# A fused attention and feed-forward kernel: a sixth VectorE exp buffer, residual rows loaded in place, and a wait that keeps GpSimd behind two-port operations

## The chip, the cores and the metric

The kernel runs on one core of one Trainium2 chip. The metric is the device time of that core in microseconds, the median of several executions. The program is built by a scheduler inside the kernel's source: it walks over streams of operations, decides which engine does what next, and emits one fixed instruction list for each engine. "Order" below means that order; it is fixed when the program is built, and it does not adapt on the chip. The program lets engines wait for each other only at semaphores.

## The reference, cut to what matters

```python
# x: 2048 rows of 512, 32 heads of 16, feed-forward width 1792, bfloat16
h  = x + attention(layernorm(x)) @ wo        # softmax over 2048 keys for each row and head
h2 = h + (gelu(n @ w_gate) * (n @ w_up)) @ w_down   # n = layernorm(h)
```

The softmax needs an exp for 32 x 2048 x 2048 scores. Cut into tiles of 128 x 512, that is 2048 tiles.

## The kernel before: the parts that matter

Most tiles go to ScalarE, two per instruction. The rest go to VectorE in groups of four: four evacuations from PSUM to 16-bit integers, and a chain of three wide operations in which GpSimd does a quarter of the product. The two factors that remain in X and W are then both multiplied with V by TensorE.

```python
# ScalarE: two tiles per exp
yield Op("act", TEXP(n), ACTF(PT[:, p0:p0 + n, :], pbank[:, b0:b0 + n, :], ACT.Exp, ...), ...)

# VectorE: one evacuation per tile (x4)
yield Op("dve", 0.603, lambda e: e.tensor_scalar(out=dXE[k % NX][:, 0, j, :], in0=pbank[:, b, :], ...))
...
# VectorE, once per group of n = 4: mask, product of 3 tiles; GpSimd: product of the 4th; second mask
yield Op("dve", ..., lambda e: e.tensor_scalar(out=W, in0=X, scalar1=0x3ff, scalar2=0xb800, ...), port=True)
yield Op("dve", ..., lambda e: e.tensor_tensor(out=W[:, 0:nd, :], in0=W[:, 0:nd, :], in1=X[:, 0:nd, :], op=ALU.mult), port=True)
yield Op("pool", TPOOL, lambda e, j=j: e.tensor_tensor(out=W[:, j, :], in0=W[:, j, :], in1=X[:, j, :], op=ALU.mult), port=True)
yield Op("dve", ..., lambda e: e.tensor_scalar(out=X, in0=X, scalar1=0x7c00, scalar2=0x8, ...), port=True)
```

`port=True` marks operations of VectorE and GpSimd that the scheduler plans one after the other, but only in its own clock. VectorE's are called two-port operations from here on; that is a name. On the chip, a GpSimd operation begins when the semaphores of its own operands allow it: all of the 369.2 us for which GpSimd is idle before its products end with VectorE's product (L1730 in the trace). GpSimd's product also lists W's first tile among its reads, so it does wait for VectorE's product of the same group; nothing keeps it behind the wide operations of other groups:

```python
def _emit(self, op, start):
    ...
    if op.port:
        self.port = end            # the plan: the next port user begins here
    ...
    tok = P.op(op.eng, fn, reads=op.reads, writes=op.writes, ...)   # semaphores: data only
```

The residual rows of x have a buffer of their own, two rows of tiles deep:

```python
xres = at("xres", [128, 2, D], BF16)
...
yield Op("dve", 0.605, lambda e: e.tensor_tensor(out=hh[:, qt, :], in0=pbank[:, b2, :], in1=xres[:, xi, :], op=ALU.add), ...)
```

Of the kernel before, what the change touches and what calls it, by code (L numbers as in the profile page):

```python
# [891 lines left out]
class Sched:  # L892
# [5 lines left out]
    def __init__(self, P, banks):  # L898
        self.P = P
        self.t = {n: 0.0 for n in P.ENGINES}  # L900
        self.done = {}
        self.streams = []
        self.banks = [(0.0, b) for b in banks]
        self.now = 0.0
        self.fill = None
        self.debt = (0.0, 0.0)
        self.pipe = 0.0
        self.lent = set()
        self.rng = random.Random(66)
        self.early = True  # L910
        self.wake = None
        self.port = 0.0
        self.room = lambda: False
        self.mode = "f"
        self.rows = [0.0] * 4
        self.due = self.INF
# [61 lines left out]
    def _emit(self, op, start):  # L978
        if op.cols:
            self.owed(start + op.dur, op.cols)  # L980
        P = self.P
        extra = op.extra() if op.extra else ()
        for tok in extra:
            start = max(start, self.done[tok] + LATS.get((tok[0], op.eng), LAT))
        self.now = max(self.now, start)
        if op.eng == "pe":
            m = "r" if op.mode == "q" else op.mode
            if m != self.mode:
                start = max(start, max(self.rows)) + TSW
            self.mode = m  # L990
        end = start + op.dur
        last = end
        if op.gs:
            at = start
            for g in op.gs:
                at = max(at, self.rows[g])
                self.rows[g] = at + TST
                at += 0.005
            end, last = at, max(self.rows)
        if op.port:  # L1000
            self.port = end
        if op.dma is not None:
            tok = P.dma(op.eng, op.fns[0], op.dma, reads=op.reads, writes=op.writes, extra_deps=extra)
            self.t[op.eng] = start + 0.5
            self.pipe = max(start + 1.5, self.pipe) + op.dur / 0.32
            self.done[tok] = self.pipe + 0.8
            if op.dma[0] in TURNS:
                self.t[op.eng] = start + 1.25
                self.done[tok] += TURNS[op.dma[0]]
        else:  # L1010
            if op.eng == "pe":
                self.wake = None
                P.group_begin("pe")
            n = len(op.fns)
            for i, fn in enumerate(op.fns):
                tok = P.op(op.eng, fn, reads=op.reads, writes=op.writes, sig=(i == n - 1), extra_deps=extra)
            if op.eng == "pe":
                P.group_end("pe")
            self.t[op.eng] = end
            self.done[tok] = last + TAIL.get(op.eng, 0.0)  # L1020
        if op.then is not None:
            op.then()
# [128 lines left out]
GS = 4  # L1151
NPOOL = 1
TPOOL = 1.11
NX = 5
GLAST = 8
AHEAD = 12
ATAIL = 8
# [10 lines left out]
XMIN = 32768.0  # L1168
# [48 lines left out]
def fast_path(nc, P, base0, ARENA, pbank, flag, A_x, A_wqkv, A_wo, B_x, B_w_gate, B_w_up, B_w_down, out):  # L1217
# [58 lines left out]
    wo_sb = at("wo_sb", [128, 4, D], BF16)  # L1276
    OnT = at("OnT", [128, 4, 4, 128], BF16)
    hn_sb = OnT[:].rearrange("p q c s -> p q (c s)")
    xres = at("xres", [128, 2, D], BF16)
    ident = at("ident", [128, 128], BF16)  # L1280
    ident32 = at("ident32", [128, 128], FP32)
    ones_bf = at("ones_bf", [128, 512], BF16)
    zero_bf = at("zero_bf", [128, 128], BF16)
    stats = at("stats", [128, NT, 6], FP32)
    mv = at("mv", [128, NT, 2], FP32)
# [83 lines left out]
        return ("x", 0, t // 2) if c == 0 else ("x", c)  # L1369

    def consts():
        yield Op("pool", 0.5, lambda e: e.memset(ones_bf[:], 1.0), writes=["ones_bf"])
        yield Op("pool", 0.3, lambda e: e.affine_select(out=ident[:], in_=ones_bf[:, 0:128], pattern=[[1, 128]], compare_op=ALU.is_equal, fill=0.0,
                                                        base=0, channel_multiplier=-1), reads=["ones_bf"], writes=["ident"])
        yield Op("pool", 0.1, lambda e: e.memset(nhalf[:], -0.5), writes=["nhalf"])
        yield Op("pool", 0.2, lambda e: e.memset(LINV[:], 2.0 ** -10), writes=[("LINV", u) for u in range(NU)])
        yield Op("pool", 0.1, lambda e: e.memset(zero_bf[:], 0.0), writes=["zero_bf"])
        yield Op("pool", 0.3, lambda e: e.tensor_copy(out=ident32[:], in_=ident[:]), reads=["ident"], writes=["ident32"])

    def ones_v():  # L1380
        yield Op("dve", 0.62, lambda e: e.memset(VA[:, :, :, 16:17], 1.0), writes=["VA_ones"])
# [2 lines left out]
    def masks():  # L1384
        yield Op("dve", 0.5, lambda e: e.memset(pbank[:, DENSE[0], :], 0.0), writes=[("pb", DENSE[0])])
        for par in range(2):
            iv = ident32[:].rearrange("p (g x i) -> p g x i", g=4, x=2)[:, :, par, :]
            yield Op("dve", 0.2, lambda e, iv=iv, par=par: e.tensor_reduce(out=qmask[:, par:par + 1], in_=iv, axis=AX.XY, op=ALU.add), reads=["ident32"], writes=[("qm", par)])
            yield Op("dve", 0.1, lambda e, par=par: e.tensor_scalar(out=qmask[:, par:par + 1], in0=qmask[:, par:par + 1], scalar1=256.0 / LN2, scalar2=None, op0=ALU.mult),
                     reads=[("qm", par)], writes=[("qm", par)])  # L1390
        yield Op("dve", 0.1, lambda e: e.tensor_scalar(out=probe[:, 0:1], in0=ident32[:, 0:1], scalar1=1e6, scalar2=XMIN, op0=ALU.add, op1=ALU.max), reads=["ident32"], writes=["probe"])


    def ln1(c):
# [198 lines left out]
    def qk():  # L1593
        nxt, an = 0, 0
        while nxt < len(TILES):
# [11 lines left out]
            while nxt in own:  # L1607
# [3 lines left out]
            yield Op("pe", TST * repeats([TILES[i][2] for i, _ in put]), mode="q", cols=143 * len(put), gs=[TILES[i][2] for i, _ in put], fns=fns, reads=rd, writes=[("pb", b) for _, b in put],  # L1611
                     gate=lambda: C["exp"] >= st - len(SLOTS) + 1 and not sch.lent & {b for _, b in put})
            sch.wake = {TILES[i][2] for i, _ in put}
            C["qk"] = st + 1
            while nxt in own:
                nxt += 1
# [39 lines left out]
    def dget():  # L1656
# [8 lines left out]
        while True:  # L1665
            yield Wait(lambda: "qkdone" in C or (room() and find()))
            if "qkdone" in C:
                return
            u, i0 = find()
            G = C["gopen"] = dict(u=u, t=[], row=range(i0, i0 + 4), k=C["gk"], conv=0)  # L1670
            for i in G["row"]:
                own[i] = ("d", G["k"])
            C["gk"] += 1
            C["dnext"] = sch.now + DGAP
            while len(G["t"]) < GS:
                b = yield Acquire(gate=lambda: pick(G) is not None and C["dout"] < DMAX - (DB if behind() else 0))
                i = pick(G)
                C["dout"] += 1
                fns, rd = scores([(i, b)])
                wk = sch.wake | {TILES[i][2]}  # L1680
                yield Op("pe", TDQ if TILES[i][2] not in sch.wake else TST, mode="r", cols=143, gs=[TILES[i][2]], fns=fns, reads=rd, writes=[("pb", b)])
                sch.wake = wk
                sch.add(dconv(G, len(G["t"]), b), -2)
                G["t"].append(i)
            close_group()
# [181 lines left out]
    def base_dl(c):  # L1867
        return T0 + first_t[c + 1] * 2 * TUNIT + 10

    def xres_loads(c):  # L1870
        for t in range(first_t[c], first_t[c + 1]):
            yield Op("sp", 0.125, lambda e, t=t: e.dma_start(out=xres[:, t % 2, :], in_=xv[:, t, :]), writes=[("xres", t % 2)], dma=("xres", t % 2),
                     gate=lambda: C["oproj"] >= t - 1)


    def copy_op(c, qt, o, i, **kw):

# [3 lines left out]

    def post(c, qt):
        cp, t = 0, first_t[c] + qt
        xi = t % 2
        hh, hT = h_c[c], hnT_c[c]
        rd = [("Otok", cp, s) for s in range(NSLOT)] + ["ident"]
        if c < NC - 1:
# [11 lines left out]
        for hf in range(2):  # L1899
            yield Op("pe", 2 * TMM, cols=1024, fns=[MM(pbank[:, b2, :], OnT[:, qt, hc, :], wo_sb[:, hc, :], hc == 0, hc == 3) for hc in (2 * hf, 2 * hf + 1)],  # L1900
                     reads=[("OH", qt), "wo"], writes=[("pb", b2)])
        dQ = P.retire(h_over[c])
        yield Op("dve", 0.605, lambda e: e.tensor_tensor(out=hh[:, qt, :], in0=pbank[:, b2, :], in1=xres[:, xi, :], op=ALU.add),
                 reads=[("pb", b2), ("xres", xi)], writes=[("h", c, qt)], extra=lambda: dQ)
        sch.release(b2)
        C["oproj"] += 1
        yield Op("dve", 0.605, lambda e: e.bn_stats(out=stats2[:, t, :], in_=hh[:, qt, :]), reads=[("h", c, qt)], writes=[("stats2", t)])
# [175 lines left out]

    def warm():
        while "qk" not in C and sch.t["pe"] < 12:
            yield Op("pe", 0.43 if sch.t["pe"] < 5.2 else 0.22, lambda e: e.matmul(pbank[:, 0, :], ident[:], ones_bf[:], start=True, stop=True), reads=["ident", "ones_bf"], writes=[("pb", 0)],
                     gate=lambda: "qk" not in C and sch.t["pe"] < 12)

    def fill_op(b):
        return Op("pe", TMM, lambda e: e.matmul(pbank[:, b, :], zero_bf[:], ones_bf[:], start=False, stop=False, skip_group_check=True), reads=["zero_bf", "ones_bf"], writes=[("pb", b)], cols=390)  # L2090

    def fill(st, nxt):

# [3 lines left out]
            op = fill_op(C["pvb"])  # L2097
        elif sch.banks:
            b = min(sch.banks)[1]
            op = Op("pe", TMM, lambda e: e.matmul(pbank[:, b, :], zero_bf[:], ones_bf[:], start=True, stop=True), reads=["zero_bf", "ones_bf"], writes=[("pb", b)], cols=390)  # L2100
        else:
            return False
        t0 = max(sch.free("pe", op), sch._ready(op))
# [75 lines left out]
```

## Time and profile before

| | before |
|---|---|
| median of four executions | 814.68 us (814.17 to 814.97) |
| exps on ScalarE, and median spacing from end to end | 778, 0.917 us |
| sum of the spacings that end in an exp | 737.2 us |
| of it above 778 x 0.9165 us ("lost between exps") | 24.1 us |
| everything else in the profiled execution of 814.4 us | 77.2 us |
| two-port operations held up by a running GpSimd operation | 64, 22.7 us |

The last rows were worked out from the trace's single instructions; a "spacing" is the time from one instruction's end to the next one's on the same engine. "Held up" means: when VectorE had finished its previous operation and the wide one had begun, a GpSimd operation was running. Where "the first 40 us" or "40 to 780 us" is said, the count starts at TensorE's first clock record, 5.3 us after the span's start here.

The chain of waits of the kernel before is followed back from the last instruction, and gives the share of the span by engine, then by line:

```profile
PE 49%; DVE 30%; ACT 10%; issue 5%; POOL 2%; DMA 0%; DVEq 0%; ACTq 0%; POOLq 0%
PE pbank L1341 31%; PE pbank L1340 14%; DVE dXE L1715 12%; ACT PT L1347 8%; DVE dXE L1730 5%; DVE dXE L1728 4%; PE pbank L2090 4%; DVE dXE L1735 4%; DVE GUT L1981 1%; POOL dXE L1732 1%; ACT GUT L1994 1%; DVE OA L1819 1%; DMA xnT<-xn_sb 0%; ACT L1347 0%; POOL xn_sb L1442 0%
```

VectorE holds 30% of the chain, nearly all of it in the operations of the exp groups (L1715, L1728, L1730, L1735). PE's shares are in large part TensorE working through its list in order. A late VectorE makes TensorE late, and ScalarE then waits for scores. The list of waits says the same (who waited for whom: us in all, times, longest):

```profile
PEld pbank L1341 <- DVE dXE L1715: 36.9, 110, 1.2
...
PEld pbank L1341 <- DVE dXE L1735: 11.5, 33, 1.2
ACT PT L1347 <- PE pbank L1341: 10.2, 21, 1.7
```

### The profile page before, as it was taken

To read this page: it belongs to the slowest core of one execution; us is meant where nothing else is said; L and a number is where in the kernel's file an instruction comes from. 1 tells how busy PE (TensorE), PEld (TensorE's weight loads), DVE (VectorE), ACT (ScalarE), POOL (GpSimd) and SP (SyncE) were. 2 spreads that over 40 slices of the span, in tenths; PEclk is the share of its full clock that TensorE was granted. 3 is DMA by queue.
4 is the path that set the end of the run, shared out by engine and by line. 5 is a ranking of instruction groups with operands and counts; after the bars stand their busy time and mean duration, and the time that the engine had idled before them with its cause. 6 is when DMAs were issued, how large, how long until landed. Compare 5 with 4: busy or idle time off the path is not lost.

```text
span 812.7 us, 20343 instructions
## 1 busy us (share of the span) xinstructions
PE 792.2 (97%) x8342; PEld 276.0 (34%) x8342; DVE 758.9 (93%) x1236; ACT 769.8 (95%) x815; POOL 246.6 (30%) x283
## 2 busy tenths in 40 slices
PE   8999999999999999999999999999999999999998
PEld 4222222222222222222233333333443343444557
DVE  8679999999999999999999999999999999999965
ACT  5899999999999999999999999999999999999972
POOL 3513345532343222122143232223224222233210
PEclk9999999999999999999999999999999999999999
DMA  6200000610021000010011000010001100110000
GB/s 208 52 8 1 7 8 7 252 48 8 7 53 28 8 7 1 8 28 21 23 46 30 11 9 21 14 28 27 8 21 28 27 8 8 28 29 16 15 22 19
DMA packets 50022, 24.33 MB, mean 30 GB/s; under 512 B 39296, under 2 KB 48896, under 8 KB 49920
## 3 DMA queue, kind: packets, MB, share of 16 engines
q1 hardware_dynamic: 49776, 22.88, 10.8%
q8 instruction: 67, 1.10, 0.5%
q14 instruction: 35, 0.29, 0.1%
q10 hardware_dynamic: 144, 0.07, 0.0%
HBM read 11.80 MB, written 2.10 MB: 17 GB/s over the span
## 4 chain that ended last, share of the span: by engine, by line
PE 49%; DVE 30%; ACT 10%; issue 5%; POOL 2%; DMA 0%; DVEq 0%; ACTq 0%; POOLq 0%
PE pbank L1341 31%; PE pbank L1340 14%; DVE dXE L1715 12%; ACT PT L1347 8%; DVE dXE L1730 5%; DVE dXE L1728 4%; PE pbank L2090 4%; DVE dXE L1735 4%; DVE GUT L1981 1%; POOL dXE L1732 1%; ACT GUT L1994 1%; DVE OA L1819 1%; DMA xnT<-xn_sb 0%; ACT L1347 0%; POOL xn_sb L1442 0%
## 5 line engine op out<-in xcount | busy, mean ns | idle before, releaser
L1347 ACT ACTIVATE PT<-pbank 128x1024 bf16<-128x1024 f32 x778 | 724.1, 1080 | 13.4 <-PE pbank L1341 10.2
L1341 PE MATMUL pbank<-QT,KT 32*128 32x512 bf16 (+1 forms) x2304 | 346.9, 359 | 8.4 <-DVE dXE L1715 3.3
L1715 DVE TENSOR_SCALAR dXE<-pbank 128x512 uint16<-128x512 f32 x492 | 323.0, 680 | 8.8 <-PE pbank L1341 6.7
L1732 POOL TENSOR_TENSOR dXE<-dXE 128x512 f16<-128x512 f16 x123 | 155.3, 1263 | 369.2 <-DVE dXE L1730 369.2
L1341 PEld LDWEIGHTS pbank<-QT,KT 32*128 32x128 bf16 x2304 | 89.2, 91 | 294.3 <-ACT PT L1347 201.9
L1341 PE MATMUL pbank<-PT,VA 128*32 128x256 bf16 (+2 forms) x2708 | 130.1, 292 | 0.0
L1730 DVE TENSOR_TENSOR dXE<-dXE 128x1536 f16<-128x1536 f16 x123 | 122.1, 993 | 1.1
L1728 DVE TENSOR_SCALAR dXE<-dXE 128x2048 uint16<-128x2048 uint16 x123 | 94.3, 767 | 0.1
L1735 DVE TENSOR_SCALAR dXE<-dXE 128x2048 uint16<-128x2048 uint16 x123 | 88.1, 720 | 5.8 <-POOL dXE L1732 4.8
L1341 PE MATMUL pbank<-dXE,VA 128*32 128x256 f16 (+2 forms) x1752 | 76.2, 289 | 2.0 <-DVE dXE L1735 1.9
L1340 PE MATMUL pbank<-hnT_c,wg_sb 128*128 128x256 bf16 (+2 forms) x392 | 70.4, 291 | 0.0
L1341 PEld LDWEIGHTS pbank<-PT,VA 128*32 128x32 bf16 x2708 | 47.4, 96 | 60.3 <-issue 57.1
L2090 PE MATMUL pbank<-ones_bf,zero_bf 128*128 128x512 bf16 x201 | 66.0, 386 | 0.0
L1340 PE MATMUL pbank<-hnT_c,wu_sb 128*128 128x256 bf16 (+2 forms) x392 | 58.0, 289 | 3.9 <-DVE GUT L2009 3.2
L1340 PE MATMUL pbank<-wd_sb,GUT 128*128 128x512 bf16 (+1 forms) x238 | 59.9, 369 | 0.0
L1841 POOL TENSOR_TENSOR Otok<-OAT,LINV 128x128 bf16<-128x128 bf16 (+2 forms) x52 | 30.1, 593 | 80.5 <-DVE LINV L1835 79.9
L1341 PEld LDWEIGHTS pbank<-dXE,VA 128*32 128x32 bf16 x1752 | 31.0, 96 | 32.2 <-issue 17.2
L1340 PE MATMUL pbank<-xnT,wqkv_sb 128*128 128x512 bf16 (+1 forms) x152 | 38.2, 349 | 0.9 <-DMA xnT<-xn_sb 0.8
L2009 DVE TENSOR_TENSOR GUT<-pbank,GUT 128x512 bf16<-128x512 f32 (+1 forms) x57 | 36.6, 670 | 1.9 <-PE pbank L1340 1.3
L1340 PEld LDWEIGHTS pbank<-hnT_c,wu_sb 128*128 128x128 bf16 x392 | 29.7, 98 | 24.1 <-issue 9.1
L1981 DVE CAST GUT<-pbank 128x512 bf16<-128x512 f32 (+1 forms) x53 | 35.4, 672 | 1.4 <-PE pbank L1340 1.3
L1533 POOL TENSOR_SCALAR QT<-QT,qmask 128x512 bf16<-128x512 bf16 x30 | 26.3, 883 | 32.7 <-DVE QT L1530 31.8
(82 smaller groups left out, 344.1 us busy)
## 6 DMA issues: line engine op xcount, KB each, us to landing
xres<-in_A_x_dram SPq DMA_DIRECT2D x16, 128.0 KB, 2.2
out_dram<-out_sb SPq DMA_DIRECT2D x15, 128.0 KB, 1.7
wg_sb<-in_B_w_gate_dram SPq DMA_DIRECT2D x1, 1792.0 KB, 7.1
wu_sb<-in_B_w_up_dram SPq DMA_DIRECT2D x1, 1792.0 KB, 11.1
wd_sb<-in_B_w_down_dram SPq DMA_DIRECT2D x1, 1792.0 KB, 15.3
x_sb<-in_A_x_dram SPq DMA_DIRECT2D x3, 512.0 KB, 9.2
wqkv_sb<-in_A_wqkv_dram SPq DMA_DIRECT2D x1, 896.0 KB, 8.5
x_sb<-in_A_x_dram SPq DMA_DIRECT2D x2, 256.0 KB, 2.9
```

The source lines that it names most:

```text
L1340: return lambda e: e.matmul(o, l, r, start=start, stop=stop)
L1341: return lambda e: e.matmul(o, l, r, start=start, stop=stop, tile_position=tile)
L1347: return lambda e: e.activation(out=o, in_=i, func=func, **kw)
L1715: yield Op("dve", 0.603, lambda e: e.tensor_scalar(out=dXE[G["k"] % NX][:, 0, j, :], in0=pbank[:, b, :], scalar1=XMIN + 1024.0 * CENTER, s ...
L1728: yield Op("dve", 0.07 + 0.133 * n, lambda e: e.tensor_scalar(out=W, in0=X, scalar1=0x3ff, scalar2=0xb800, op0=ALU.bitwise_and, op1=ALU.bi ...
L1730: yield Op("dve", 0.066 + 0.267 * nd, lambda e: e.tensor_tensor(out=W[:, 0:nd, :].bitcast(F16), in0=W[:, 0:nd, :].bitcast(F16), in1=X[:, 0 ...
L1732: yield Op("pool", TPOOL, lambda e, j=j: e.tensor_tensor(out=W[:, j, :].bitcast(F16), in0=W[:, j, :].bitcast(F16), in1=X[:, j, :].bitcast( ...
L1735: yield Op("dve", 0.07 + 0.133 * (h1 - h0), lambda e, h0=h0, h1=h1: e.tensor_scalar(out=X[:, h0:h1, :], in0=X[:, h0:h1, :], scalar1=0x7c00 ...
L1841: yield Op("pool" if turned else "dve", 0.15 + 0.55 / len(slots) if turned else 0.06 + 0.28 / len(slots), lambda e, o4=o4, lx=lx, o_ap=o_a ...
L1981: yield Op("dve", 0.07 + 0.001042 * n * CHUNKS[c], lambda e: e.tensor_copy(out=o_ap, in_=i_ap), reads=[("pb", b)], writes=keys, extra=dE)
L2009: yield Op("dve", 0.07 + 0.001042 * n * CHUNKS[c], lambda e: e.tensor_tensor(out=o_ap, in0=u_ap, in1=o_ap, op=ALU.mult), reads=[("pb", b)] ...
L2090: return Op("pe", TMM, lambda e: e.matmul(pbank[:, b, :], zero_bf[:], ones_bf[:], start=False, stop=False, skip_group_check=True), reads=[ ...
```

## The change

It has three intents: give VectorE a sixth buffer for exp groups; find the memory for it by loading the residual rows straight into the buffer that later takes x1 (the first sum), and by shrinking two constants; and stop GpSimd from starting before a two-port VectorE operation that the plan had put ahead of it. The seed of the scheduler's random order changes too. The core of the diff:

```diff
-        self.rng = random.Random(66)
+        self.rng = random.Random(31)
+        self.port_tok = self.dve_tok = None
...
+        if op.eng == "pool" and self.port_tok:
+            extra = list(extra) + [self.port_tok]      # one more semaphore to wait for
...
+            if op.eng == "dve":
+                if op.port:
+                    self.port_tok = self.dve_tok       # the operation AHEAD of the two-port one
+                self.dve_tok = tok
...
-NX = 5
+NX = 6
...
-    xres = at("xres", [128, 2, D], BF16)
-    ident32 = at("ident32", [128, 128], FP32)
-    ones_bf = at("ones_bf", [128, 512], BF16)
+    ones_bf = at("ones_bf", [128, 128], BF16)          # read four times over where 512 are needed
...
     def xres_loads(c):
+        yield Wait(lambda: ...)                          # until the chunk's scores have all been issued (and a second condition)
-            yield Op("sp", ..., e.dma_start(out=xres[:, t % 2, :], in_=xv[:, t, :]), ...)
+            yield Op("sp", ..., e.dma_start(out=h_c[c][:, t - first_t[c], :], in_=xv[:, t, :]), ...)
...
-        yield Op("dve", ..., e.tensor_tensor(out=hh[:, qt, :], in0=pbank[:, b2, :], in1=xres[:, xi, :], op=ALU.add), ...)
+        yield Op("dve", ..., e.tensor_tensor(out=hh[:, qt, :], in0=pbank[:, b2, :], in1=hh[:, qt, :], op=ALU.add), ...)
```

More of the change, by code (lines that the diff above doesn't have):

```diff
@@ L1278, in fast_path @@
     hn_sb = OnT[:].rearrange("p q c s -> p q (c s)")
-    xres = at("xres", [128, 2, D], BF16)
     ident = at("ident", [128, 128], BF16)
-    ident32 = at("ident32", [128, 128], FP32)
-    ones_bf = at("ones_bf", [128, 512], BF16)
+    ones_bf = at("ones_bf", [128, 128], BF16)
+    ones4 = ones_bf[:].unsqueeze(1).broadcast_to([128, 4, 128])
+    quads = lambda b: pbank[:, b, :].rearrange("p (x i) -> p x i", x=4)
     zero_bf = at("zero_bf", [128, 128], BF16)
@@ L1371, in consts @@
     def consts():
-        yield Op("pool", 0.5, lambda e: e.memset(ones_bf[:], 1.0), writes=["ones_bf"])
+        yield Op("pool", 0.25, lambda e: e.memset(ones_bf[:], 1.0), writes=["ones_bf"])
         yield Op("pool", 0.3, lambda e: e.affine_select(out=ident[:], in_=ones_bf[:, 0:128], pattern=[[1, 128]], compare_op=ALU.is_equal, fill=0.0,
@@ L1377, in consts @@
         yield Op("pool", 0.1, lambda e: e.memset(zero_bf[:], 0.0), writes=["zero_bf"])
-        yield Op("pool", 0.3, lambda e: e.tensor_copy(out=ident32[:], in_=ident[:]), reads=["ident"], writes=["ident32"])
     def ones_v():
@@ L1386, in masks @@
         for par in range(2):
-            iv = ident32[:].rearrange("p (g x i) -> p g x i", g=4, x=2)[:, :, par, :]
-            yield Op("dve", 0.2, lambda e, iv=iv, par=par: e.tensor_reduce(out=qmask[:, par:par + 1], in_=iv, axis=AX.XY, op=ALU.add), reads=["ident32"], writes=[("qm", par)])
+            iv = ident[:].rearrange("p (g x i) -> p g x i", g=4, x=2)[:, :, par, :]
+            yield Op("dve", 0.2, lambda e, iv=iv, par=par: e.tensor_reduce(out=qmask[:, par:par + 1], in_=iv, axis=AX.XY, op=ALU.add), reads=["ident"], writes=[("qm", par)])
             yield Op("dve", 0.1, lambda e, par=par: e.tensor_scalar(out=qmask[:, par:par + 1], in0=qmask[:, par:par + 1], scalar1=256.0 / LN2, scalar2=None, op0=ALU.mult),
                      reads=[("qm", par)], writes=[("qm", par)])
-        yield Op("dve", 0.1, lambda e: e.tensor_scalar(out=probe[:, 0:1], in0=ident32[:, 0:1], scalar1=1e6, scalar2=XMIN, op0=ALU.add, op1=ALU.max), reads=["ident32"], writes=["probe"])
+        yield Op("dve", 0.1, lambda e: e.tensor_scalar(out=probe[:, 0:1], in0=ident[:, 0:1], scalar1=1e6, scalar2=XMIN, op0=ALU.add, op1=ALU.max), reads=["ident"], writes=["probe"])
     def ln1(c):
@@ L1613, in qk @@
             sch.wake = {TILES[i][2] for i, _ in put}
+            for i in mine:
+                tiles_of(i)
             C["qk"] = st + 1
@@ L1682, in dget @@
                 sch.wake = wk
+                tiles_of(i)
                 sch.add(dconv(G, len(G["t"]), b), -2)
@@ L1868, in base_dl, with tiles_of, hkey @@
         return T0 + first_t[c + 1] * 2 * TUNIT + 10
+    def tiles_of(i):
+        C["iss", units[unit_of(i)][0]] = C.get(("iss", units[unit_of(i)][0]), 0) + 1
     def xres_loads(c):
+        yield Wait(lambda: C.get(("iss", c), 0) == 64 * NSLOT // per(c) and C["down"] >= h_off[c][2])
+        over = P.retire(h_over[c])
         for t in range(first_t[c], first_t[c + 1]):
-            yield Op("sp", 0.125, lambda e, t=t: e.dma_start(out=xres[:, t % 2, :], in_=xv[:, t, :]), writes=[("xres", t % 2)], dma=("xres", t % 2),
-                     gate=lambda: C["oproj"] >= t - 1)
+            k = ("h", c, t - first_t[c])
+            yield Op("sp", 0.125, lambda e, t=t: e.dma_start(out=h_c[c][:, t - first_t[c], :], in_=xv[:, t, :]), writes=[k], dma=("xres", t % 2),
+                     gate=lambda: C["oproj"] >= t - 1, extra=lambda: list(over) + (P.retire([hkey(t - 2)]) if t >= 2 else []))
+    def hkey(t):
+        c = max(c for c in range(NC) if first_t[c] <= t)
+        return "h", c, t - first_t[c]
     def copy_op(c, qt, o, i, **kw):
@@ L1883, in post @@
         cp, t = 0, first_t[c] + qt
-        xi = t % 2
         hh, hT = h_c[c], hnT_c[c]
@@ L1902, in post @@
         dQ = P.retire(h_over[c])
-        yield Op("dve", 0.605, lambda e: e.tensor_tensor(out=hh[:, qt, :], in0=pbank[:, b2, :], in1=xres[:, xi, :], op=ALU.add),
-                 reads=[("pb", b2), ("xres", xi)], writes=[("h", c, qt)], extra=lambda: dQ)
+        yield Op("dve", 0.605, lambda e: e.tensor_tensor(out=hh[:, qt, :], in0=pbank[:, b2, :], in1=hh[:, qt, :], op=ALU.add),
+                 reads=[("pb", b2), ("h", c, qt)], writes=[("h", c, qt)])
         sch.release(b2)
@@ L2085, in warm @@
         while "qk" not in C and sch.t["pe"] < 12:
-            yield Op("pe", 0.43 if sch.t["pe"] < 5.2 else 0.22, lambda e: e.matmul(pbank[:, 0, :], ident[:], ones_bf[:], start=True, stop=True), reads=["ident", "ones_bf"], writes=[("pb", 0)],
+            yield Op("pe", 0.43 if sch.t["pe"] < 5.2 else 0.22, lambda e: e.matmul(quads(0), ident[:], ones4, start=True, stop=True), reads=["ident", "ones_bf"], writes=[("pb", 0)],
                      gate=lambda: "qk" not in C and sch.t["pe"] < 12)
     def fill_op(b):
-        return Op("pe", TMM, lambda e: e.matmul(pbank[:, b, :], zero_bf[:], ones_bf[:], start=False, stop=False, skip_group_check=True), reads=["zero_bf", "ones_bf"], writes=[("pb", b)], cols=390)
+        return Op("pe", TMM, lambda e: e.matmul(quads(b), zero_bf[:], ones4, start=False, stop=False, skip_group_check=True), reads=["zero_bf", "ones_bf"], writes=[("pb", b)], cols=390)
     def fill(st, nxt):
@@ L2099, in fill @@
             b = min(sch.banks)[1]
-            op = Op("pe", TMM, lambda e: e.matmul(pbank[:, b, :], zero_bf[:], ones_bf[:], start=True, stop=True), reads=["zero_bf", "ones_bf"], writes=[("pb", b)], cols=390)
+            op = Op("pe", TMM, lambda e: e.matmul(quads(b), zero_bf[:], ones4, start=True, stop=True), reads=["zero_bf", "ones_bf"], writes=[("pb", b)], cols=390)
         else:
```

## The prediction

> **What bounds the kernel now.** I read four views in this order: the totals, the 40 slices, the groups and the timelines round one stall.
>
> ```profile
> PE 792.2 (97%) x8342; PEld 276.0 (34%) x8342; DVE 758.9 (93%) x1236; ACT 769.8 (95%) x815; POOL 246.6 (30%) x283
> ...
> DVE  8679999999999999999999999999999999999965
> ACT  5899999999999999999999999999999999999972
> ...
> L1347 ACT ACTIVATE PT<-pbank 128x1024 bf16<-128x1024 f32 x778 | 724.1, 1080 | 13.4 <-PE pbank L1341 10.2
> L1715 DVE TENSOR_SCALAR dXE<-pbank 128x512 uint16<-128x512 f32 x492 | 323.0, 680 | 8.8 <-PE pbank L1341 6.7
> L1732 POOL TENSOR_TENSOR dXE<-dXE 128x512 f16<-128x512 f16 x123 | 155.3, 1263 | 369.2 <-DVE dXE L1730 369.2
> ...
> L1730 DVE TENSOR_TENSOR dXE<-dXE 128x1536 f16<-128x1536 f16 x123 | 122.1, 993 | 1.1
> L1728 DVE TENSOR_SCALAR dXE<-dXE 128x2048 uint16<-128x2048 uint16 x123 | 94.3, 767 | 0.1
> L1735 DVE TENSOR_SCALAR dXE<-dXE 128x2048 uint16<-128x2048 uint16 x123 | 88.1, 720 | 5.8 <-POOL dXE L1732 4.8
> ```
>
> The softmax has 2048 score tiles of 128x512. ScalarE does 778 exps of two tiles, VectorE with GpSimd does 123 groups of four (778x2 + 123x4 = 2048). Both are full from slice 3 to slice 38. PE's 97% is padded: 201 of its matmuls only add zeros. So the end is set by ScalarE's chain of exps and by whatever holds it up.
>
> A recorded exp (mean 1080 ns) includes time queued behind its predecessor; I therefore measured, in the trace's single instructions, the spacing from one end to the next on ScalarE. Its median is 0.917 us. The 778 spacings that end in an exp sum to 737.2 us; 778 x 0.9165 is 713.0. So **24.1 us are lost between exps**: 5.5 in the first 40 us, 18.6 later. Everything else (start, gelu, table loads, tail) is 814.8 - 737.2 = 77.6 us. The most that any repair of stalls can bring is those 24.1 us.
>
> Measured the same way, VectorE's two 2048-wide operations take 0.60 us and the 1536-wide product 0.867 us when undisturbed. Sixty-four times one of these operations (or a like one) is ready to begin while a GpSimd operation is running, and these cost 22.7 us extra. One of them:
>
> ```profile
> 457.84 0.69 DVE L1728 TENSOR_SCALAR dXE<-dXE 128x2048 uint16<-128x2048 uint16 x1
> 458.56 1.79 DVE L1730 TENSOR_TENSOR dXE<-dXE 128x1536 f16<-128x1536 f16 x1
> ...
> 458.00 1.54 POOL L1732 TENSOR_TENSOR dXE<-dXE 128x512 f16<-128x512 f16 x1 [6.43 <-DVE dXE L1730]
> ...
> 461.65 4.74 ACT L1347 ACTIVATE PT<-pbank 128x1024 bf16<-128x1024 f32 x5 [0.61 <-PE pbank L1341]
> ```
>
> GpSimd's product, released at 458.00, runs until 459.54. VectorE's product, which should end near 459.4, lasts until 460.35. TensorE, in order behind VectorE's evacuations, then delivers scores late, and ScalarE stands still for 0.61 us before 461.65. The chain of waits runs through exactly this operation:
>
> ```profile
> 458.56 1.79 DVE dXE L1730
> 460.35 0.61 DVE dXE L1715
> 460.96 0.05 issue
> 461.01 1.48 PE pbank L1341 x21
> ```
>
> [...] the 19 cases in which the 2048-wide mask (L1728) met a running product (L1732) cost 10.1 us, 0.53 each, nearly the operation's own 0.60; without overlap 96 of them lost 0.24 us in all. [...]
>
> **The change part by part.**
>
> 1. *GpSimd behind two-port operations.* Each GpSimd operation now also waits for the VectorE operation before the last two-port operation that the kernel's scheduler had already placed. It is then released when that two-port operation may begin, not earlier, and should queue behind it. I logged the order in which the scheduler of the kernel before places instructions: in 61 of the 64 overlaps GpSimd's operation was placed after the VectorE operation it delayed, so the new wait covers them; they cost 21.7 us of VectorE. In the build of the changed kernel, GpSimd instructions with a VectorE wait go from 188 to 206, and many of the others wait for a later one.
>
>  How much of 21.7 us reaches ScalarE? Two estimates. First, of the 18.6 us lost after the first 40 us, 13.6 fall within 7 us after a stretched operation (excess over 0.1 us) and 4.8 elsewhere (the rest in gaps too small to count). Those windows cover 55% of the time, so at the rate of the uncovered 45% (4.8 us in 338, 0.0143 per us) they would hold 5.8 us anyhow; 13.6 - 5.8 = 7.8 us is the stretches' share. Second, the chain of waits holds 26 stretched operations with 10.8 us excess, an upper limit, since a second chain takes over when one is shortened. I take **-7 us**.
>
> 2. *Sixth buffer.* By the order of instructions the changed kernel has 124 groups and 776 exps (2048 again). Two exps fewer: **-1.8 us** of ScalarE. One more group costs VectorE 2.40 + 0.60 + 0.867 + 0.60 = 4.47 us, paid out of the 21.7 it no longer loses. The buffer changes no operation's length; it only loosens when a group may begin, and the group count shows how little the scheduler makes of it.
>
> 3. *Residual rows into the buffer that takes x1.* Sixteen loads of 128 KB, 2.2 us each, as before, but a chunk's loads now wait until its last scores have read the Q it lies on (mostly a wait for PE). Those scores come before the last exps, products, transposes (2.5 and 2.4 us DMAs) and projection of the chunk. For the last chunk in the kernel before, scores end at 785.0 and the addition is at 792.34: 7.3 us for a 2.2 us load. Hidden, **0**. The addition's operand moves, not its size (680 ns).
>
> 4. *Smaller constants.* A 0.29 us cast and part of a 0.53 us memset leave GpSimd at the start, where the loads of x and the statistics decide. **0**. Matmuls that now read 128 ones four times over have the same size.
>
> 5. *New random order.* The seed changes, so all engines' orders shift. In the tail, after the last scores, TensorE has 14 instead of 44 gate matmuls of the sixth chunk left (30 x 0.056 us = 1.7 less) and 32 more value products (0.56 more). TensorE is busy 19.8 of the last 23 us, so I take **-1 us**.
>
> 6. *Against it.* GpSimd's products start up to 0.87 us later, and L1735 waits for them: 4.8 us in 6 waits now. The scheduler already counts the port as taken in turn and places L1735 accordingly: **+0.5 us**.
>
> Sum: -7 - 1.8 - 1 + 0.5 = -9.3; 814.8 - 9.3 = **805.5 us**.
>
> **The rivals.** (a) *The stall moves to the other side*: GpSimd late, so VectorE waits at L1735, TensorE waits for the group, and little is won. For it: that wait exists. Against it: VectorE usually has other groups' evacuations between, and six buffers help. It would leave 810 to 813. (b) *VectorE's lateness was what filled ScalarE's gaps nearly alone*: with it gone, most of the 18.6 us return; for it stands the chain's 10.8 us; against it the 4.8 us with no stretch nearby. It would make 796 to 800. (c) *The residual loads block the SP queue*, which is in order, and transposes queue behind a load that waits for PE. Transposes feed only the feed-forward work, which has slack except at the tail; 1 to 3 us at worst. (d) *The seed's luck*: either order could have some 3 us more or fewer planned stalls.
>
> **Range and chances.** 800 to 811.5: the lower end is (b) in part, the upper end (a) with bad luck. Faster by over 2% needs 798.5 or less: with 776 exps, 711.2 + 77.6 - 1 = 787.8 leaves only 10.7 us of lost time, 5.5 of them in the first 40 us. I give it 6%; slower by over 2% 0.5%, as no work is added to ScalarE.
>
> **What would show it.** Mean of L1728 falling from 767 to about 690 ns and L1730 from 993 to about 950; POOL's L1732 lengthening above 1263 ns as it waits in the queue instead; VectorE operations delayed by a running GpSimd operation falling from 64 to under 15; lost time between exps falling to about 17 us; VectorE's wait for L1732 staying under 10 us; VectorE idle growing, not ScalarE. If stretches vanish but lost time stays above 21 us, step 1's share was wrong; if L1735's wait grows past 15 us, rival (a).

The sum of this forecast came to -9.3 us, so 805.5 us. The sentence about 19 and 96 masks is measured: in the kernel before, a first mask that met a running GpSimd product lost 0.53 us (10.1 us in 19), one that met no GpSimd operation next to nothing (0.24 us in 96). Measured end to end, an evacuation of 512 from PSUM takes 0.598 us (its record has a mean of 680 ns), and four of them are the 2.40 us of a group. The 0.056 us of a gate matmul and the 0.56 us of 32 value products are measured in the same trace: 104 spacings between gate matmuls of 128 columns have a median of 0.056, and the 32 value products after the last scores take 0.561 in all.

## The result, and the profile after

The changed kernel takes 804.33 us (median of four: 804.28, 804.31, 804.34 and one of 806.0, which comes up again at the end). The kernel before takes 814.68. The ratio of the two is 0.9879, with a 95% interval of 0.9865 to 0.9894. Ratios are the mean time of one kernel's fast runs over that of the other's in the same rounds, so not quite the ratio of the medians. It is 1.2% faster.

The totals and the groups of the changed kernel (line, engine, operation, shapes, count | busy us, mean ns | idle before, and what ended it):

```profile
PE 784.3 (98%) x8308; PEld 276.0 (34%) x8347; DVE 746.5 (93%) x1243; ACT 764.4 (95%) x813; POOL 257.2 (32%) x283
...
L1354 ACT ACTIVATE PT<-pbank 128x1024 bf16<-128x1024 f32 x776 | 718.6, 1090 | 9.4 <-PE pbank L1348 7.4
...
L1741 POOL TENSOR_TENSOR dXE<-dXE 128x512 f16<-128x512 f16 x124 | 162.5, 1311 | 361.8 <-DVE dXE L1739 288.3
...
L1739 DVE TENSOR_TENSOR dXE<-dXE 128x1536 f16<-128x1536 f16 x124 | 117.9, 951 | 1.0
L1744 DVE TENSOR_SCALAR dXE<-dXE 128x2048 uint16<-128x2048 uint16 x124 | 85.9, 695 | 6.1 <-POOL dXE L1741 5.2
L1737 DVE TENSOR_SCALAR dXE<-dXE 128x2048 uint16<-128x2048 uint16 x124 | 85.3, 688 | 0.2
```

VectorE has one group more to do and is busy 12 us less. The first mask fell from 767 to 688 ns, the product from 993 to 951, and GpSimd's product grew from 1263 to 1311. Part of the waiting has moved to GpSimd, which holds only 1% of the chain of waits.

The chain of waits of the changed kernel, by engine:

```profile
PE 77%; ACT 12%; issue 4%; DVE 2%; POOL 1%; DMA 1%; SPq 0%; ACTq 0%; DVEq 0%; POOLq 0%
```

VectorE's share of the chain went from 30% to 2%. VectorE is nearly as busy as before (93%), but it no longer sets the end.

The timeline shows the mechanism from the other side. Compare the stretch of 458 us shown in the prediction. Here GpSimd's product is released by the evacuation (L1724) ahead of the mask, not by its data; it begins at 464.23, 0.16 us after the mask, and is the one that waits:

```profile
463.46 0.68 DVE L1724 TENSOR_SCALAR dXE<-pbank 128x512 uint16<-128x512 f32 x1
464.07 0.68 DVE L1737 TENSOR_SCALAR dXE<-dXE 128x2048 uint16<-128x2048 uint16 x1
464.67 0.68 DVE L1724 TENSOR_SCALAR dXE<-pbank 128x512 uint16<-128x512 f32 x1
...
464.23 1.53 POOL L1741 TENSOR_TENSOR dXE<-dXE 128x512 f16<-128x512 f16 x1 [5.25 <-DVE dXE L1724]
```

The mask keeps its 0.68 us and GpSimd's product takes 1.53 in place of some 1.15 (the median of the 124 products is 1.157).

| | before | changed |
|---|---|---|
| exps | 778 | 776 |
| sum of spacings ending in an exp | 737.2 | 727.7 |
| lost between exps | 24.1 | 16.5 |
| everything else in the profiled execution | 77.2 | 76.6 |
| two-port operations held up, and their cost | 64, 22.7 us | 5, 2.4 us |

So of the 10.1 us between these two profiled executions (814.4 and 804.31), 7.6 are lost time that went, 1.8 are the two exps (2 x 0.917), and 0.6 lie in the rest.

### The profile page after: what moved, and what is told of

Same layout as the page of the kernel before. It is cut to its first block, busy times and chain, and to the rows that moved or that the text cites. A ratio compares the mean times of both kernels' runs of the same rounds, so it can differ in the third digit from the quotient of the medians.

```text
span 802.6 us, 20316 instructions
## 1 busy us (share of the span) xinstructions
PE 784.3 (98%) x8308; PEld 276.0 (34%) x8347; DVE 746.5 (93%) x1243; ACT 764.4 (95%) x813; POOL 257.2 (32%) x283
## 4 chain that ended last, share of the span: by engine, by line
PE 77%; ACT 12%; issue 4%; DVE 2%; POOL 1%; DMA 1%; SPq 0%; ACTq 0%; DVEq 0%; POOLq 0%
PE pbank L1348 49%; PE pbank L1347 24%; ACT PT L1354 11%; PE pbank L2109 5%; DVE dXE L1724 1%; ACT GUT L2013 1%; DMA xnT<-xn_sb 1%; DVE dXE L1739 0%; POOL xn_sb L1448 0%; DVE dXE L1744 0%; DVE GUT L2028 0%; DVE dXE L1737 0%; ACT L1354 0%; POOL rstd L1434 0%; POOL htmp L1445 0%
## 5 line engine op out<-in xcount | busy, mean ns | idle before, releaser
L1348 PE MATMUL pbank<-QT,KT 32*128 32x512 bf16 (+1 forms) x2304 | 340.8, 359 | 5.6 <-ACT PT L1354 1.8
L1724 DVE TENSOR_SCALAR dXE<-pbank 128x512 uint16<-128x512 f32 x496 | 326.8, 682 | 13.0 <-PE pbank L1348 10.8
L1741 POOL TENSOR_TENSOR dXE<-dXE 128x512 f16<-128x512 f16 x124 | 162.5, 1311 | 361.8 <-DVE dXE L1739 288.3
L1739 DVE TENSOR_TENSOR dXE<-dXE 128x1536 f16<-128x1536 f16 x124 | 117.9, 951 | 1.0
L1744 DVE TENSOR_SCALAR dXE<-dXE 128x2048 uint16<-128x2048 uint16 x124 | 85.9, 695 | 6.1 <-POOL dXE L1741 5.2
L1737 DVE TENSOR_SCALAR dXE<-dXE 128x2048 uint16<-128x2048 uint16 x124 | 85.3, 688 | 0.2
L1347 PE MATMUL pbank<-wd_sb,GUT 128*128 128x512 bf16 (+1 forms) x214 | 54.9, 367 | 3.2 <-issue 3.0
L1850 POOL TENSOR_TENSOR Otok<-OAT,LINV 128x128 bf16<-128x128 bf16 (+2 forms) x52 | 31.8, 623 | 66.7 <-DVE dXE L1724 25.2
L1539 POOL TENSOR_SCALAR QT<-QT,qmask 128x512 bf16<-128x512 bf16 x30 | 28.6, 955 | 37.1 <-DVE QT L1536 26.1
```

The lines of the kernel that those rows point to most:

```text
L1347: return lambda e: e.matmul(o, l, r, start=start, stop=stop)
L1348: return lambda e: e.matmul(o, l, r, start=start, stop=stop, tile_position=tile)
L1724: yield Op("dve", 0.603, lambda e: e.tensor_scalar(out=dXE[G["k"] % NX][:, 0, j, :], in0=pbank[:, b, :], scalar1=XMIN + 1024.0 * CENTER, s ...
L1737: yield Op("dve", 0.07 + 0.133 * n, lambda e: e.tensor_scalar(out=W, in0=X, scalar1=0x3ff, scalar2=0xb800, op0=ALU.bitwise_and, op1=ALU.bi ...
L1739: yield Op("dve", 0.066 + 0.267 * nd, lambda e: e.tensor_tensor(out=W[:, 0:nd, :].bitcast(F16), in0=W[:, 0:nd, :].bitcast(F16), in1=X[:, 0 ...
L1744: yield Op("dve", 0.07 + 0.133 * (h1 - h0), lambda e, h0=h0, h1=h1: e.tensor_scalar(out=X[:, h0:h1, :], in0=X[:, h0:h1, :], scalar1=0x7c00 ...
```

## The experiments

Eleven kernels were run, all correct. The question was less whether the total was right than whether the terms were: the waits, the sixth buffer, the move of the residual rows and the seed all came at once. Two kinds of kernel keep them apart. One kind keeps the **order of every instruction** and only adds or removes GpSimd's extra semaphore wait. That wait carries no data, so it can be taken away without a race, and the traces of such a pair show the same instructions in the same order on every engine (apart from some 40 matmul records of 8,300 that are missing from some of the traces). The other kind changes one size and lets the scheduler form a new order.

### The wait alone, on the kernel before

```diff
+        if op.eng == "pool" and self.port_tok:
+            extra = list(extra) + [self.port_tok]
...
+            if op.eng == "dve":
+                if op.port:
+                    self.port_tok = self.dve_tok
+                self.dve_tok = tok
```

> The kernel before with only the extra GpSimd wait; the order of all instructions is unchanged (778 exps, 123 groups, nothing moved). Theory (the waits end the stretching of VectorE's two-port operations, and about a third of the 21.7 us reaches ScalarE): 807.5 us, between 805 and 810; VectorE operations delayed by a running GpSimd operation fall from 64 to under 10, L1728 from 767 to about 690 ns, lost time between exps from 24 to about 17 us. Rival (the gain comes from the sixth buffer and the new order; the stall only moves to GpSimd's side): 813 to 815.5, with VectorE's wait for GpSimd's product above 10 us.

Measured: 809.08 us against 814.55 for the kernel before beside it, 5.5 us less. Held-up operations fell from 64 to 11, and lost time from 24.1 to 18.4 us. The theory's time was met (809.08 in 805 to 810) and its lost time nearly (18.4 for "about 17"); the eleven are over its "under 10". One of the rival's marks showed up as well. VectorE's second mask now waits more than twice as long for GpSimd's product:

```profile
DVE dXE L1742 <- POOL dXE L1739: 10.9, 15, 1.6
```

In the kernel before this wait was 4.8 us in 6 times. So with five buffers a part of the gain is handed to the other side, as rival (a) of the prediction had it, though only a part.

### The changed kernel without the wait

```diff
         for tok in extra:
             start = max(start, ...)          # the plan still counts the wait
+        if op.eng == "pool" and self.port_tok:
+            extra = extra[:-1]               # the semaphore is not emitted
```

> The changed kernel without the extra GpSimd wait; the order of all instructions is kept (776 exps, 124 groups). Theory: the stretches come back (40 or more delayed operations) and the time rises by 5 to 9 us, to 811 us (809 to 813.5). Rival (buffer and order did it): 804 to 806.

Measured: 810.76 us, 6.4 above the changed kernel. Forty-eight operations are held up again, lost time is back at 23.3 us, and VectorE is back on the chain. Its product and first mask, and the chain by engine:

```profile
PE 59%; DVE 28%; ACT 3%; issue 3%; POOL 2%; DMA 1%; SPq 0%; DVEq 0%; POOLq 0%; ACTq 0%
...
L1741 DVE TENSOR_TENSOR dXE<-dXE 128x1536 f16<-128x1536 f16 x124 | 121.7, 981 | 1.0
L1739 DVE TENSOR_SCALAR dXE<-dXE 128x2048 uint16<-128x2048 uint16 x124 | 92.6, 747 | 0.2
```

This is what the theory expected (809 to 813.5). The same instructions in the same order, with one kind of wait fewer, and VectorE goes from 2% to 28% of the chain: the stretches, and 6.4 us, are the missing wait's doing. That a running GpSimd operation stretches VectorE's is shown by the two pairs that differ in the wait alone (held-up operations 48 to 5 here, 64 to 11 above) and by the prediction's 19 stretched and 96 unstretched masks. By what means it does so was not shown. The run also shows that buffer, order and memory moves without the wait are worth 814.6 - 810.8 = 3.8 us.

### Five buffers in the changed kernel

```diff
-NX = 6
+NX = 5
```

> The changed kernel with five exp buffers instead of six, the waits kept; the scheduler then forms 121 groups and 782 exps. Theory (the buffer is worth what its groups take off ScalarE): 6 exps more at 0.917 us = 5.5 us, so 809.5 us (808 to 811.5), lost time between exps as in the changed kernel, 15 to 19 us. Rival (the buffer shortens waits rather than adding groups): lost time above 20 us and the time above 812. Rival (the buffer does nothing): 804 to 806.

Measured: 812.16 us as a median, but with a wide scatter (810.64 to 813.65). Three of the four executions have a mean granted clock of 0.997 to 0.999, and only the one of 810.64 has 1.0. That one is 6.3 us above the changed kernel, close to the 5.5 us that six more exps cost, and within the expected 808 to 811.5; the median is above it, and just above the 812 of the first rival, whose other mark (over 20 us lost) is not met. The profile, taken in one of the disturbed executions, has 17.6 us lost. VectorE's wait for GpSimd's product is 10.2 us in 11 waits, against 5.2 in 9 with six buffers:

```profile
DVE dXE L1744 <- POOL dXE L1741: 10.2, 11, 1.8
```

So the buffer's worth is mostly its three groups. A smaller wait for GpSimd goes with it.

### The old seed in the changed kernel

```diff
-        self.rng = random.Random(31)
+        self.rng = random.Random(66)
```

> The changed kernel with the old random order (seed 66); also 124 groups and 776 exps. Theory (the seed is luck of a few us at most): 804.3 plus or minus 2.5 us. Rival (the new order carries much of the gain): 808 us or more.

Measured: 807.73 us, 3.4 us slower, with the same 124 groups. The expectation (804.3 plus or minus 2.5) missed by 0.9 us, and the rival's mark of 808 was missed by 0.3. Lost time is 18.7 in place of 16.5, and the rest 77.8 in place of 76.6. The seed is worth more than I gave it: an order with the same counts can differ by over 3 us.

### The kernel before with the new seed, with and without the wait

```diff
-        self.rng = random.Random(66)
+        self.rng = random.Random(31)
```

and the same again with the wait added as in the first experiment. Both have 121 groups and 782 exps, in one and the same order.

> The kernel before with the new seed and the extra GpSimd wait, five buffers and the old place of the residual rows: 121 groups, 782 exps. Theory: as the changed kernel with five buffers, 809.5 us (807.5 to 812), since the place of the residual rows and the constants count nothing. Rival (moving the residual rows costs or gains time by itself): more than 2 us from the changed kernel with five buffers.

> The kernel before with the new seed alone: the same order as the run with the extra wait, without it; 121 groups, 782 exps. Theory: 4 more exps than before at 0.917 us, stretches as before: 818.5 us (816 to 821), and 5 to 9 us above the same order with the wait. Rival (seed 31 is simply the better order): below 814.

Measured: 811.66 us with the wait, as expected, and 1.0 us from the undisturbed execution of the changed kernel with five buffers (810.64). Those two differ in the place of the residual rows and the constants and have the same number of exps. Without the wait it is 813.06 us: the wait is worth only 1.4 us here, not 5 to 9, and the run is 3 us below the range that I had given. It lies below 814, the mark of the rival that seed 31 is simply the better order: without the wait it is 1.5 us faster than the kernel before in spite of four exps more, since only 18.9 us are lost in place of 24.1. With the wait and five buffers, however, seed 31 is 2.6 us slower than seed 66 (811.66 against 809.08), so "better" holds for no seed by itself. The small worth of the wait needed an explanation. My first one was how full VectorE is: with 121 groups it is idle for 37 us in the middle of the run (40 to 780 us), against 23 us in the kernel before, so stretches might be taken up by idle time.

### The residual rows and constants alone

The kernel before with the memory moves, but five buffers, the old seed and no wait.

```diff
 # kept of the change: loads into h_c, small constants; taken back:
-NX = 6
+NX = 5
-        self.rng = random.Random(31)
+        self.rng = random.Random(66)
-        if op.eng == "pool" and self.port_tok:
-            extra = list(extra) + [self.port_tok]
```

> The kernel before with only the residual rows in the buffer that takes x1 and the small constants; five buffers, old seed, no extra wait. The scheduler forms 121 groups, 782 exps. Theory: no effect but 4 more exps, 818.5 us (816 to 821). Rival (moved loads are late and hold up the queue): above 822 us, with waits of the SP queue for PE ahead of transposes on the chain.

Measured: 816.73 us, 2.2 us slower than the kernel before, within the expected range. It has 782 exps (3.7 us more) and 18.8 us lost. Everything outside the exps grew from 77.2 to 81.3 us, and no load shows as the cause: in the tail the addition waits 0.17 us, and for TensorE, not for a transfer:

```profile
790.96 0.69 DVE L1920 TENSOR_TENSOR h_c<-pbank,h_c 128x512 bf16<-128x512 f32 x1 [0.17 <-PE pbank L1345]
```

The last exp ends at 784.8 and the span at 815.0, 30.2 us later, against 26.3 in the kernel before (786.4 to 812.7). Part of this is work: TensorE is busy for 25.6 us after the last exp, against 23.3. The other 1.6 us are idle time of TensorE: while VectorE adds and normalises the last rows, TensorE waits, and these operations of VectorE lie on the chain, as they do not in the kernel before:

```profile
790.96 0.70 DVE h_c L1920
...
791.68 0.71 DVE stats L1924
...
792.60 1.02 DVE GUT L1998 x2
...
793.68 0.41 DVE OnT L1929
```

### Waiting for the end of the two-port operation

The changed kernel in its own order, but GpSimd waits for the two-port operation itself.

```diff
-                    self.port_tok = self.dve_tok
+                    self.port_tok, self.port_end = self.dve_tok, tok
...
+        if op.eng == "pool" and self.port_tok:
+            extra = extra[:-1] + [self.port_end]
```

> The changed kernel in its own order, but GpSimd waits for the end of the two-port operation itself, not for the operation ahead of it. Theory (what matters is that GpSimd does not begin first): delayed operations stay under 10 and the time within 1.5 us of the changed kernel, perhaps 0.5 us more as GpSimd loses the length of a semaphore's way each time. Rival (the earlier release matters because GpSimd's work is on the chain): 807 us or more, with VectorE's wait for GpSimd's product growing from 5 us to over 15.

Measured: 808.76 us, 4.4 us slower. I had expected at most 1.5. Held-up operations stay few (8, 1.4 us), so stretches are not the cause. Comparing the two traces product by product shows it. In the changed kernel a GpSimd product that lies in wait ends 1.01 us after the end of the two-port operation (that is the tenth and the 25th percentile). If it is released by a semaphore at that end, it ends 1.23 us after it. The difference, the expectation's "semaphore's way", is 0.22 us. It does not concern all 124 products: about half of them end later, and the differences add up to 15 us. TensorE's wait for the finished group grows with it, from 6.7 us in 24 waits in the changed kernel (first line) to 11.3 in 35:

```profile
PEld pbank L1348 <- DVE dXE L1744: 6.7, 24, 0.7
...
PEld pbank L1350 <- DVE dXE L1746: 11.3, 35, 0.9
```

VectorE's own wait for GpSimd grew only from 5.2 to 6.8 us, so the mark that the rival named for itself is not met; its time is. VectorE is back at 26% of the chain without any stretch to speak of. That GpSimd is released one operation early is worth 4.4 us in this order, more than the choice of seed (3.4).

### Is it VectorE's idle time that decides what the wait is worth?

Two more pairs test the explanation of the 1.4 us. Both are kernels from above, with the wait taken away and the order kept, by the same edit as in the second experiment.

> The changed kernel with the old seed, its order kept, without the extra GpSimd wait: 124 groups, 776 exps. New theory (what a stretch costs depends on how full VectorE is; with 124 groups it has little idle time): 5 to 7.5 us above the same order with the wait (807.7), so 812.7 to 815.2. Rival (the worth of the wait varies by chance from order to order): 809 to 812.

> The changed kernel with five buffers (121 groups, 782 exps), its order kept, without the extra GpSimd wait. New theory (with 121 groups VectorE has 37 to 45 us of idle time in the middle, which takes up most stretches): 1 to 3 us above the same order with the wait (812.2), so 813 to 815.2. Rival (the wait is worth the same in every order): 817 to 819.

Measured: 812.38 us, 4.7 above its partner and 0.3 below the range (and 0.4 above the rival's); and 818.46 us, 6.3 above its partner of 812.16, within the range of the rival (817 to 819). These two ran on another chip than their partners; the kernel before took 814.44 us there and 814.55 on the first, so the chips differ by little. The second refutes the idea. With 121 groups and VectorE idle for 36 us in the middle, the wait was still worth about 6 us. (Both members of this pair have clock dips; the least disturbed executions are 817.58 at 0.999 and 810.64 at 1.0.) What does separate the pairs is how much of the stretching lies on the chain of waits. I summed the excess of all two-port operations on the chain that were stretched by over 0.1 us:

| order | groups | without wait | with wait | worth | stretch on the chain, without / with | VectorE waits for GpSimd's product, without / with |
|---|---|---|---|---|---|---|
| before | 123 | 814.55 | 809.08 | 5.5 | 10.8 / 3.0 | 4.8 / 10.9 |
| before, seed 31 | 121 | 813.06 | 811.66 | 1.4 | 4.7 / 0.9 | 4.6 / 9.2 |
| changed, five buffers | 121 | 818.46 | 812.16 | 6.3 | 7.7 / 0.1 | 3.0 / 10.2 |
| changed, seed 66 | 124 | 812.38 | 807.73 | 4.7 | 8.1 / 1.1 | 5.8 / 7.4 |
| changed | 124 | 810.76 | 804.33 | 6.4 | 9.2 / 0.0 | 4.2 / 5.2 |

In four of the pairs the time gained is 0.67 to 0.83 of the stretch that left the chain; in the order with 1.4 us it is 0.37, and that order had the least stretch on the chain. Why so little of it lay there is a property of that one order, and I have no run that explains it further. The last column gives a pattern too. With five buffers the wait makes VectorE stand 4.6 to 7.2 us longer for GpSimd's product, with six only 1.0 to 1.6. That the sixth buffer is the reason is likely, since it is what those pairs share, but no run changed the buffers without changing the order, and the shares of the wait and of the order can't be told apart there.

### An attempt at a better order

```diff
-        self.rng = random.Random(31)
+        self.rng = random.Random(118)
-DBUSY = 2.0
+DBUSY = 2.5
```

> The changed kernel with seed 118 and a longer pause between groups while feed-forward work is behind (2.5 in place of 2.0): again 124 groups and 776 exps. Chosen among some 200 orders by the kernel's own plan. If the plan is right to within a microsecond: 803 to 805, a little below the changed kernel; if orders differ by luck as the seeds 31 and 66 did (3.4 us): 804 to 808.

Measured: 806.32 us as a median, so the second of the two expectations. The four executions took 805.0, 805.5 and 807.4 us at a mean granted clock of 1.0, and 807.1 at 0.998; the slow one at 1.0 stays unexplained. In the profiled execution of 805.0 us lost time is 15.8 us, a little less than in the changed kernel, but the rest is 78.0 in place of 76.6. It beats the kernel before, not the changed one; none of the runs does.

## Why the prediction was right

The prediction of 805.5 us is 1.2 us above the measured 804.33. It is held here against the terms of its sum, since a sum can be right by luck.

1. **GpSimd behind two-port operations: -7 us predicted.** The two runs that change nothing else gave -5.5 (order of before) and -6.4 (order of the changed kernel). Of the two estimates behind the term, the window count gave 7.8 and the chain an upper limit of 10.8. The chain's figure held as a limit in all five pairs. Held-up operations fell to 5 where "under 15" was said, the first mask to 688 ns ("about 690"), the product to 951 ("about 950"), and lost time to 16.5 us ("about 17").
2. **Sixth buffer: -1.8 us predicted.** The count of 776 exps is exact, and 2 x 0.917 us follows. What failed is the sentence that the group count shows how little the scheduler makes of the buffer. That compared a lucky order with five buffers (123 groups) with one with six. At the new seed, five buffers give 121 groups, and the buffer is worth three groups, six exps, 6.3 us in the undisturbed execution. Building both kernels with twelve seeds gave 121.7 groups on average for the kernel before and 123.3 for the changed one (a rebuild with the seeds 1 to 12 gave 121.75 and 123.17). So the buffer did more, and the loss of a lucky order hid part of it. The 6.3 us of seed 31 flatter it in turn: 1.6 groups are 3.2 exps, some 2.9 us by estimate.
3. **Residual rows: 0 predicted.** No wait for a residual load appears in VectorE's waits of the changed kernel, the addition keeps its length (679 ns before, 678 after, of 16), and the pair with equal counts (811.66 and 810.64) is 1.0 us apart. Right as far as the runs tell; orders scatter by more than that.
4. **Constants: 0 predicted.** The time lost in the first 40 us is 5.5 before and 5.8 after. The matmuls that only add zeros, which read 128 ones four times over in the changed kernel, take 386 ns in both (201 and 204 of them).
5. **New order: -1 us predicted.** Everything outside the exps fell by 0.6 us. (The prediction's 77.6 us set the trace of an execution of 814.4 us against a median of 814.8; within one execution it is 77.2.) But in the changed kernel the seed as a whole is worth 3.4 us, of which 2.2 are lost time: the term was mis-sized. Three measured steps lead from the kernel before to the changed one: the wait -5.5 (814.55 to 809.08), then the sixth buffer with the memory moves -1.4 (to 807.73), then the seed -3.4 (to 804.33). Another path splits the gain otherwise: the seed -1.5, the wait -1.4, buffer and moves -7.3 (813.06, 811.66, 804.33). So the parts have no worth of their own, and that the prediction's terms add up so well is in part luck: the wait and the new order were set at 7 and 1, and came out at 5.5 and 3.4 on the path that takes the wait first.
6. **Against it: +0.5 us predicted.** VectorE's wait for GpSimd grew by 0.4 us (4.8 to 5.2). In the three orders with five buffers it grew by 4.6 to 7.2. Rival (a) was held off here, and not in general.

Rival (b) would have needed nearly all lost time to go: 10.7 us remained outside the first 40. Of rival (c) the mechanism appeared, but no cost: the SP queue stood 47.6 us in three waits for TensorE ahead of residual loads (10.6, 21.0 and 16.0) and issued nothing else in them, and yet the only transfer on the chain is a transpose at 34.8 us, before the first of these loads.

## What to carry to other kernels

A plan that puts operations of two engines one after the other is only a plan until a semaphore enforces it: here 64 operations were held up for 22.7 us under such a plan. Look for two-port VectorE operations whose records stretch while a GpSimd operation is running, and sum the excess that lies on the chain of waits, which was an upper limit of what the repair brought in all five pairs. Release GpSimd one operation early, so that its operation is already under way when VectorE's ends: its product then ended 1.01 us after VectorE's operation, in place of 1.23 us when a semaphore released it at that end, and the kernel with the later release took 4.4 us more. And when a change comes with a new random order, run the old order with each part, or the new order without it: here the seed alone moved the time by 3.4 us one way in the changed kernel, a third of the whole gain, and by 2.6 us the other way in the kernel before with the wait.

## The granted clock and the stray executions

In the profiled run of the changed kernel with five buffers, TensorE pauses 2.21 us for VectorE, and then the granted clock (the column after POOL's count) halves for about 3.4 us, worked out from (0.18 + 0.50 + 0.17) x 2 us / 0.5. Its partner without the wait has the same 2.21 us of idle time between 300 and 320 us, and a mean clock of 0.94 there and 0.98 in the 20 us after. What decides is not shown: that partner has a second dip, with a mean of 0.91 between 720 and 740 us, where TensorE is idle for only 1.11 us in all, and in the kernel before with seed 31 a pause of 1.8 us brought none (the clock stays at 1.00 in every stretch). Such dips are a likely reason for some of the stray executions, by the author's estimate: the changed kernel's 806.0 us came with a mean clock of 0.998, its other three at 1.0 with 804.3. They are not the reason for all: the attempt at a better order has one of 807.4 us at 1.0. The first line below is of the timeline, the others are of the table by stretches:

```profile
314.33 1.04 PE L1347 MATMUL pbank<-hnT_c,wu_sb 128*128 128x512 bf16 x4 [2.21 <-DVE GUT L2028]
...
314.00:316.00 2.00, 1.67 (x7) 0.69 (x8) 2.00 (x5) 2.00 (x1) 0.99 (x1) 0.82 0.00 0
316.00:318.00 2.00, 2.00 (x6) 0.73 (x5) 1.59 (x4) 1.97 (x3) 0.00 (x0) 0.50 0.00 0
318.00:320.00 2.00, 2.00 (x14) 0.73 (x16) 1.37 (x3) 1.81 (x2) 0.00 (x0) 0.83 0.00 0
```
